# Start addresses of the second layer's SBUF tiles: from 96 bytes past a multiple of 256 to multiples of 256

## The chip, the cores and the metric

The kernel runs on one core of a Trainium2 chip. The metric is device time in microseconds (us) of one execution; the lower the better. TensorE (PE) multiplies matrices. It takes two operands from the on-chip memory SBUF: a stationary one, the weights, which a weight load (PEld) puts in place ahead of the matmul, and a moving one, which streams past it. VectorE (DVE) and ScalarE (ACT) do the elementwise work, GpSimd (POOL) a little of it, and SyncE (SP) issues the transfers (DMA).

## The reference

An attention with a decaying state, then two feed-forward layers on its output, all in float32:

```
B, H, S, D = 4, 8, 768, 48;  tokens 3072, d_model 384, d_ff 2048
for t:   y_t   = r_t @ (state + (u*k_t) v_t^T);   state = w * state + k_t v_t^T
layer 1: h = x @ w_in;  g = max(h, 0) + alpha * min(h, 0);  x2 = g @ w_out
layer 2: h = x2 @ w_in; g = h * tanh(softplus(h));          out = g @ w_out
```

## The kernel before, in words

**Blocks and slots.** The 3072 tokens form six blocks of 512 (NCH = 6). A layer goes through its 2048 inner features in sixteen tiles of 128 (NF = 16). One block with one feature tile is a slot, so each layer has 96 slots. In a slot TensorE forms h for 128 features and 512 tokens (`emit_h`, L229) and later adds the slot's share of the output to accumulators (`mA_out`, L612, in layer 1; `mB_out`, L730 and L732, in layer 2).

**Nine and nine.** Each float32 operand is held as a high and a low part (`hi`, `lo`), and a product is three matmuls: high by high, high by low, low by high. With 384 = 3 x 128 input features, h takes nine matmuls of 128 x 512, and the output takes nine too. Only the last block of layer 2 turns the output product round: there the parts of g are the weights, `w_out` is the moving operand with 384 columns, and a slot has twelve of them (L730).

**Order.** Layer 1 runs slot by slot along the places of a table, with the attention of later tokens between the slots (L433 to L485: many small matmuls, a batch of them every four slots). Layer 2 runs in pairs: the h of two slots, then the outputs of the two slots that lie four slots back (LAG_B = 4). `mish` (L671) puts six ACT and five DVE operations of each slot between h and the output. The places of the instructions are the same in both kernels.

**Homes of the tiles.** A tile gets its place in SBUF from a pool, in the order of creation. Pool `per` lives throughout: the block inputs `x`, the weight tiles `w0` to `w12` of both layers, `w13` to `w15` of layer 1, and the parts `ghi`, `glo` of g in layer 1. Pool `att` holds the attention's tiles. At the end of layer 1 `fin_open` (L627) closes `att` and puts pool `fin` over the same bytes: three constants for ACT's bias operand, the layer 2 tiles `w13`, `w14`, `w15` (W_OWN = 13, L193), the parts of g in four buffers each (`ghiB`, `gloB`, L592), and the tiles `a`, `b`, `s2`, `c`, `s3` and `oo` that TensorE doesn't read. The last slots of layer 1 (from G_3 = 86 on) already write their g to `ghiB` and `gloB`.

A tile of one column takes 32 bytes of a partition. Three of them stand at the start of `fin`, so all that follows starts 96 bytes past a multiple of 256.

Of the kernel before, what the change touches and what calls it, by code (L numbers as in the profile page):

```python
# [21 lines left out]
F32 = mybir.dt.float32  # L22
# [7 lines left out]
B, H, S, D = 4, 8, 768, 48  # L30
# [3 lines left out]
NPR = H // 2  # L34
# [3 lines left out]
PR = 112  # L38
# [93 lines left out]
MK = (32.0 / 768398401.0) ** 0.5  # L132
# [4 lines left out]
def attention_and_two_ff(ctx: ExitStack, tc, rkT, nat, wT, ub, consts, w1, w2, alphaT, out):  # L137
# [8 lines left out]
    att = att_ctx.enter_context(tc.tile_pool(name="att", bufs=1))  # L146
# [88 lines left out]
    oma = per.tile([128, NF], F32, name="oma")  # L235
    wt = att.tile([PR, NPR], F32, name="wt")
    w64 = att.tile([PR, NPR], F32, name="w64")
    cst = att.tile([128, 2 * C], F32, name="cst")
    ubt = att.tile([128, DM], F32, name="ubt")
    ident = cst[:, 0:128]  # L240
# [44 lines left out]

    RK = per.tile([PR, 2, NPR, C], F32, tag="w1", name="RK")
    RKs = att.tile([PR, 2, NPR, C], F32, name="RKs")
    uw = att.tile([PR, NPR, 2], F32, name="uw")
    w96 = att.tile([PR, NPR], F32, name="w96")
    Kn = att.tile([128, 2, NPR, 2, D], F32, name="Kn")  # L290
    T = att.tile([PR, B, NPR, 64], F32, name="T")
    def tables():
# [78 lines left out]
        dve.tensor_tensor(out=rk, in0=rk, in1=w.unsqueeze(2).to_broadcast([PR, 2 * NPR, 2, HC]), op=ALU.mult)  # L371

    def new_c(u):
        return att.tile([128, H, 1], F32, tag="cc", name="cc", bufs=2)

    def c_first(u):

        rk = inp[u][0]
        m = new("g")[0:PR].rearrange("d (p s) -> d p s", p=NPR)
        dve.tensor_tensor(out=m, in0=rk[:, 0], in1=rk[:, 1], op=ALU.mult)  # L380
        y = yt_t[u] = bank(*(("yt",), ("acc1",), ("h", 2), ("h", 2))[u])
        t = y[:, KC * C:KC * C + H]
        for p in range(NPR):
            pe.matmul(t[:, 2 * p:2 * p + 2], m[:, p, :], uw[:, p, :], start=True, stop=True)
        c_t[u] = None, new_c(u)
        act.activation(out=c_t[u][1][:, :, 0].rearrange("s (q p) -> s q p", q=2),
                       in_=t.rearrange("s (p q) -> s q p", q=2), func=AF.Copy)

    def prep_c(u):
        n = inp[u][1]  # L390
        c_t[u] = n[:, 0].rearrange("s (h d) -> s h d", h=H), new_c(u)
        pool.tensor_tensor(out=n[:, 0], in0=n[:, 0], in1=ubt, op=ALU.mult)
        pool.tensor_tensor(out=n[:, 0], in0=n[:, 0], in1=n[:, 1], op=ALU.mult)
# [231 lines left out]
    fin = {}  # L625

    def fin_open():  # L627
        att_ctx.close()
        fin["p"] = ctx.enter_context(tc.tile_pool(name="fin", bufs=1))
        for nm, v in (("half", 0.5), ("m1", -1.0), ("m575", 575.0 * MK)):  # L630
            fin[nm] = fin["p"].tile([128, 1], F32, name=nm)
            pool.memset(fin[nm], v)

    def load_x2(j):
# [15 lines left out]
    v = {}  # L650
# [194 lines left out]
    with tc.manual_schedule():  # L845
# [65 lines left out]
        for f in range(NF):  # L911
# [3 lines left out]
            at(s + 2.69, w_join, (1, f))  # L915
            at(s + 2.69, w2_store, f)
        at(80.69, fin_open)
        at(78.7, load_x2, 0)
        when = [(13, 82.72), (14, 83.4), (0, 83.69), (1, 84.69), (2, 85.69), (15, 86.4), (3, 86.69), (4, 87.69), (5, 88.69),
# [98 lines left out]
```

## Time and profile before

| | |
|---|---|
| median of three runs | 884.35 us (883.03 to 884.73) |
| the profiled execution's own time | 883.32 us |
| its span in the trace | 881.4 us |
| PE busy | 872.5 us, 99% of the span |
| DVE, ACT, POOL busy | 637.8, 608.7, 97.3 us |
| granted TensorE clock | full in all 40 slices of the page |

The span is what the trace covers, from the first instruction to the last; 1.9 us of the profiled execution's time lie around it. Matmuls overlap in the trace: one of 512 columns is recorded with some 0.39 us, and the next starts long before that is over. What a matmul costs is therefore read from start to start.

### The profile page before, as it was taken

To read this page: it belongs to the slowest core of one execution; us is meant where nothing else is said; L and a number is where in the kernel's file an instruction comes from. 1 tells how busy PE (TensorE), PEld (TensorE's weight loads), DVE (VectorE), ACT (ScalarE), POOL (GpSimd) and SP (SyncE) were. 2 spreads that over 40 slices of the span, in tenths; PEclk is the share of its full clock that TensorE was granted. 3 is DMA by queue.
4 is the path that set the end of the run, shared out by engine and by line. 5 is a ranking of instruction groups with operands and counts; after the bars stand their busy time and mean duration, and the time that the engine had idled before them with its cause. 6 is when DMAs were issued, how large, how long until landed. Compare 5 with 4: busy or idle time off the path is not lost.

```text
span 881.4 us, 16867 instructions
## 1 busy us (share of the span) xinstructions
PE 872.5 (99%) x6460; PEld 721.7 (82%) x6460; DVE 637.8 (72%) x1029; ACT 608.7 (69%) x1150; POOL 97.3 (11%) x119
## 2 busy tenths in 40 slices
PE   9899999999999999999999999999999999999998
PEld 8788888888888888888888888888888888888897
DVE  7799856656657566544656887887887887887876
ACT  2677745455445544544555998998998998998886
POOL 3633122111122111100002000000000000000000
PEclk9999999999999999999999999999999999999999
DMA  8975474255444426212620200110110110100101
GB/s 308 277 241 155 133 188 138 85 159 163 137 132 138 140 88 215 64 57 88 189 89 19 108 1 0 27 47 1 28 45 1 27 46 1 25 12 1 24 14 36
DMA packets 65839, 80.40 MB, mean 91 GB/s; under 512 B 39712, under 2 KB 52960, under 8 KB 65760
## 3 DMA queue, kind: packets, MB, share of 16 engines
q1 hardware_dynamic: 65200, 79.24, 30.1%
q8 instruction: 50, 0.82, 0.4%
q14 instruction: 29, 0.24, 0.1%
q10 hardware_dynamic: 560, 0.10, 0.1%
HBM read 61.16 MB, written 15.73 MB: 87 GB/s over the span
## 4 chain that ended last, share of the span: by engine, by line
PE 97%; DVE 1%; ACT 1%; DMA 0%; issue 0%; POOL 0%; DVEq 0%; ACTq 0%; POOLq 0%
PE h L229 44%; PE acc L612 23%; PE sc L732 8%; PE acc L732 8%; PE yt L732 4%; PE acc L730 3%; PE acc L564 2%; PE sc L433 1%; PE sc L730 1%; PE h L464 1%; PE yt L485 1%; PE sc L478 1%; PE yt L464 1%; DMA x2d<-xo 0%; DVE g L380 0%
## 5 line engine op out<-in xcount | busy, mean ns | idle before, releaser
L229 PE MATMUL h<-x,w 128*128 128x512 f32 x1728 | 418.5, 391 | 2.1 <-DVE x L158 1.0
L229 PEld LDWEIGHTS h<-x,w 128*128 128x128 f32 x1728 | 323.9, 188 | 74.5 <-ACT w L155 1.2
L612 PE MATMUL acc<-ghi,w 128*128 128x512 f32 x516 | 175.1, 394 | 0.0
L580 ACT ACTIVATE m<-h 128x512 f32<-128x512 f32 x96 | 57.1, 595 | 91.2 <-PE h L229 91.1
L612 PEld LDWEIGHTS acc<-ghi,w 128*128 128x128 f32 x516 | 96.8, 188 | 21.3
L582 DVE SCALAR_TENSOR_TENSOR g<-m,oma,h 128x512 f32<-128x512 f32 x96 | 71.5, 745 | 57.4 <-ACT m L580 56.4
L155 ACT ACTIVATE ghi<-g 128x512 fp32r<-128x512 f32 x86 | 54.1, 629 | 79.4 <-PE acc L612 43.0
L612 PE MATMUL acc<-glo,w 128*128 128x512 f32 x258 | 100.4, 389 | 0.0
L158 DVE TENSOR_TENSOR glo<-g,ghi 128x512 fp32r<-128x512 f32 x86 | 59.3, 689 | 52.5 <-ACT ghi L155 52.4
L669 DVE SCALAR_TENSOR_TENSOR a<-ghi,h 128x512 f32<-128x512 f32 x96 | 66.0, 687 | 43.0 <-ACT ghi L666 36.1
L677 ACT ACTIVATE m<-h 128x512 f32<-128x512 f32 x96 | 56.3, 587 | 42.3 <-PE h L229 42.3
L669 DVE SCALAR_TENSOR_TENSOR g<-s,c 128x512 f32<-128x512 f32 x95 | 65.1, 686 | 25.3 <-ACT s L666 25.2
L158 DVE TENSOR_TENSOR gloB<-g,ghiB 128x512 fp32r<-128x512 f32 x105 | 71.9, 685 | 7.2 <-ACT ghiB L155 7.2
L666 ACT ACTIVATE ghi<-m,half 128x512 f32<-128x512 f32 x96 | 69.6, 725 | 3.2
L155 ACT ACTIVATE ghiB<-g 128x512 fp32r<-128x512 f32 x105 | 64.8, 617 | 9.2 <-PE acc L612 7.3
L732 PE MATMUL sc<-ghiB,w 128*128 128x512 f32 x192 | 68.1, 395 | 0.0
L666 ACT ACTIVATE glo<-ghi,m 128x512 f32<-128x512 f32 x96 | 68.0, 709 | 0.1
L666 ACT ACTIVATE s<-s,m 128x512 f32<-128x512 f32 x96 | 68.0, 709 | 0.0
L666 ACT ACTIVATE s<-glo,m 128x512 f32<-128x512 f32 x96 | 68.0, 708 | 0.0
L669 DVE SCALAR_TENSOR_TENSOR b<-ghi,a 128x512 f32<-128x512 f32 x96 | 67.2, 701 | 0.1
L669 DVE SCALAR_TENSOR_TENSOR c<-glo,b 128x512 f32<-128x512 f32 x95 | 65.0, 684 | 0.0
L732 PE MATMUL acc<-ghiB,w 128*128 128x512 f32 x192 | 63.0, 395 | 0.0
(193 smaller groups left out, 1167.7 us busy)
## 6 DMA issues: line engine op xcount, KB each, us to landing
wrawr<-in_w SPq DMA_DIRECT2D x24, 768.0 KB, 6.0
nat<-in_nat SPq DMA_DIRECT2D x40, 288.0 KB, 4.3
w2d<-wj SPq DMA_DIRECT2D x16, 384.0 KB, 2.6
wraw<-w2d SPq DMA_DIRECT2D x16, 384.0 KB, 3.0
rk<-in_rkT SPq DMA_DIRECT2D x40, 128.0 KB, 2.9
x2d<-xo SPq DMA_DIRECT2D x6, 768.0 KB, 3.2
x<-x2d SPq DMA_DIRECT2D x6, 768.0 KB, 4.4
rk<-in_rkT SPq DMA_DIRECT2D x40, 96.0 KB, 2.6
```

What stands on the lines that cost most here:

```text
L155: act.activation(out=hi, in_=src, func=AF.Copy)
L158: eng.tensor_tensor(out=lo, in0=src, in1=hi.bitcast(F32), op=ALU.subtract)
L229: pe.matmul(h, w_in(layer, f, a, c), x[:, b, c, :], start=(k == 0), stop=(k == 3 * KC - 1))
L464: pe.matmul(y[i][64 * q:64 * q + 64, p * HC:(p + 1) * HC], T[ROWS[h], 2 * bp + i, k, :], pair[i][ROWS[h], 0, k, t], start=(r == 0 and not ...
L580: act.activation(out=m, in_=hA[s], func=AF.Relu, scale=-1.0)
L582: dve.scalar_tensor_tensor(out=g, in0=m, scalar=oma[:, f:f + 1], in1=hA.pop(s), op0=ALU.mult, op1=ALU.add)
L612: pe.matmul(acc[0][c], w_out(0, f, a)[:, c * 128:(c + 1) * 128], g[b], start=(f == 0 and k == 0), stop=(f == NF - 1 and k == 2))
L666: act.activation(out=out, in_=in_, func=AF.Square, scale=scale, bias=fin[bias])
L669: dve.scalar_tensor_tensor(out=out, in0=in0, scalar=scalar, in1=in1, op0=op0, op1=ALU.mult)
L677: act.activation(out=bnew("t", n), in_=v["h", n], func=AF.Tanh, scale=0.5)
L730: pe.matmul(acc[1][t][:, :DM], g[a][:, t * C:(t + 1) * C], w_out(1, f, b), **se)
L732: pe.matmul(acc[1][t], w_out(1, f, a)[:, t * 128:(t + 1) * 128], g[b], **se)
```

## The change

Three places of the code change the bytes at which tiles start; no instruction is added, taken away or moved on any engine, and no wait changes. In `att`, the small tiles `uw` and `w96` are created earlier and `w96` is 40 columns wide instead of 4 (only the first 4 are used); the small tiles `cc` have four columns a head instead of one. In `fin`, the three bias constants are columns of one tile of 64 columns (256 bytes).

```diff
     w64 = att.tile([PR, NPR], F32, name="w64")
+    uw = att.tile([PR, NPR, 2], F32, name="uw")
+    w96 = att.tile([PR, 40], F32, name="w96")[:, 0:NPR]
     cst = att.tile([128, 2 * C], F32, name="cst")
...
-    uw = att.tile([PR, NPR, 2], F32, name="uw")
-    w96 = att.tile([PR, NPR], F32, name="w96")
...
-        return att.tile([128, H, 1], F32, tag="cc", name="cc", bufs=2)
+        return att.tile([128, H, 4], F32, tag="cc", name="cc", bufs=2)[:, :, 0:1]
...
-        for nm, v in (("half", 0.5), ("m1", -1.0), ("m575", 575.0 * MK)):
-            fin[nm] = fin["p"].tile([128, 1], F32, name=nm)
+        t = fin["p"].tile([128, 64], F32, name="biases")
+        for n, (nm, v) in enumerate((("half", 0.5), ("m1", -1.0), ("m575", 575.0 * MK))):
+            fin[nm] = t[:, n:n + 1]
             pool.memset(fin[nm], v)
```

The first byte of the tiles within a partition, as the two built programs have it, and what is left of it after division by 256 and by 512:

| tiles | before | mod 256 | mod 512 | changed | mod 256 | mod 512 |
|---|---|---|---|---|---|---|
| `x`, `w0` to `w12`, layer 1's `w13` to `w15`, `ghi`, `glo` | 141568 (`x`) | 0 | 256 | the same | 0 | 256 |
| layer 2's `w13` (and `w14`, `w15`) | 176480 | 96 | 352 | 176640 | 0 | 0 |
| `ghiB`, `gloB` (first buffer) | 194912 | 96 | 352 | 195072 | 0 | 0 |
| attention: `rk`, `nat`, `T` (`rk`) | 190336 | 128 | 384 | 190464 | 0 | 0 |
| attention: `Ah` | 220608 | 192 | 448 | 220928 | 0 | 256 |
| `cst` | 176448 | 64 | 320 | 176640 | 0 | 0 |

The slices that TensorE takes of these tiles begin whole multiples of 512 bytes further on in the feed-forward layers (128 columns of 4 bytes), so that they have the same remainders as their tiles.

## Rows read from the trace of the kernel before

**Rows 1.** The page: the span, and PE's busy time, share and instructions.

```profile
span 881.4 us, 16867 instructions
...
PE 872.5 (99%) x6460; PEld 721.7 (82%) x6460; DVE 637.8 (72%) x1029; ACT 608.7 (69%) x1150; POOL 97.3 (11%) x119
```

**Rows 2.** Who waited for whom from 440 us on: total, times, longest.

```profile
ACT m L677 <- PE h L229: 42.3, 47, 3.0
...
PEld acc L730 <- DVE gloB L158: 0.2, 1, 0.2
```

**Rows 3.** Windows: stretch, its length, busy time and instructions of each engine, clock.

```profile
403.30:444.08 40.78, 40.78 (x181) 33.77 (x180) 24.11 (x33) 21.71 (x35) 0.00 (x0) 1.00 0.43 140
444.08:823.32 379.24, 379.24 (x1639) 307.67 (x1638) 299.75 (x467) 325.58 (x541) 6.53 (x4) 1.00 0.11 27
823.32:881.40 58.08, 54.53 (x283) 50.11 (x281) 42.28 (x68) 45.70 (x77) 0.00 (x0) 0.99 0.12 27
```

**Rows 4.** Timeline of PE, end of layer 1: start, length, matmuls merged.

```profile
431.84 2.20 PE L229 MATMUL h<-x,w 128*128 128x512 f32 x9
...
433.88 0.39 PE L612 MATMUL acc<-ghi,w 128*128 128x512 f32 x1
...
435.92 2.20 PE L229 MATMUL h<-x,w 128*128 128x512 f32 x9
...
444.08 0.40 PE L612 MATMUL acc<-ghiB,w 128*128 128x512 f32 x1
...
446.19 4.28 PE L229 MATMUL h<-x,w 128*128 128x512 f32 x18
...
450.31 0.40 PE L612 MATMUL acc<-ghiB,w 128*128 128x512 f32 x1
```

**Rows 5.** Timeline of PE in layer 2, around a change of blocks.

```profile
594.24 4.36 PE L229 MATMUL h<-x,w 128*128 128x512 f32 x18
...
598.44 0.39 PE L732 MATMUL acc<-ghiB,w 128*128 128x512 f32 x1
...
602.64 4.28 PE L229 MATMUL h<-x,w 128*128 128x512 f32 x18
...
606.76 0.40 PE L732 MATMUL acc<-ghiB,w 128*128 128x512 f32 x1
...
617.38 0.39 PE L732 MATMUL acc<-gloB,w 128*128 128x512 f32 x1
...
618.74 0.39 PE L732 MATMUL acc<-gloB,w 128*128 128x512 f32 x1
```

**Rows 6.** Timeline of PE in layer 2's last block.

```profile
823.32 0.51 PE L730 MATMUL acc<-w,ghiB 128*128 128x384 f32 x2
...
827.49 4.28 PE L229 MATMUL h<-x,w 128*128 128x512 f32 x18
...
831.61 0.51 PE L730 MATMUL acc<-w,ghiB 128*128 128x384 f32 x2
...
852.35 4.34 PE L229 MATMUL h<-x,w 128*128 128x512 f32 x18
...
856.53 0.52 PE L730 MATMUL acc<-w,ghiB 128*128 128x384 f32 x2
...
860.77 4.38 PE L229 MATMUL h<-x,w 128*128 128x512 f32 x18
...
864.99 0.52 PE L730 MATMUL acc<-w,ghiB 128*128 128x384 f32 x2
```

**Rows 7.** Timeline of PE in layer 1, from the end of an attention batch.

```profile
264.21 0.50 PE L612 MATMUL acc<-ghi,w 128*128 128x512 f32 x1
264.55 0.39 PE L612 MATMUL acc<-glo,w 128*128 128x512 f32 x1
...
266.40 2.21 PE L229 MATMUL h<-x,w 128*128 128x512 f32 x9
```

**Rows 8.** Groups of ACT from 500 to 600 us, and two of the page: busy, mean ns, idle before.

```profile
L677 ACT ACTIVATE m<-h 128x512 f32<-128x512 f32 x24 | 14.1, 587 | 9.6 <-PE h L229 9.6
...
L155 ACT ACTIVATE ghi<-g 128x512 fp32r<-128x512 f32 x86 | 54.1, 629 | 79.4 <-PE acc L612 43.0
...
L155 ACT ACTIVATE ghiB<-g 128x512 fp32r<-128x512 f32 x105 | 64.8, 617 | 9.2 <-PE acc L612 7.3
```

## The prediction

> **What bounds the kernel now.** I read the page first: PE is busy 872.5 of 881.4 us [rows 1]. Then the list of waits: from 440 us on no row of it has PE's matmuls waiting; one weight load waits once, for 0.2 us, while ACT waits 42.3 us for PE [rows 2]. So from there to nearly the end the time is the number of matmuls times what one costs from start to start. The clock column is 1.00 throughout both long stretches [rows 3], so nothing is to be had from the clock. The question is what a matmul costs, and where it costs more.
>
> For that I read PE's timeline, start to start. At the end of layer 1, from 431.84 to 435.92 us, one slot's nine h matmuls and nine output matmuls take 2.04 + 2.04 = 4.08 us [rows 4], which is 4.08 / 18 = 226.7 ns each. The stretch up to 444.08 keeps that pace: 180 weight loads in 40.78 us [rows 3] (that count is exact; the count of matmuls has one more, which overlaps the edge). At 444.08 the first output product reads `ghiB` and `gloB`, and this one alone takes until 446.19: 2.11 us instead of 2.04 [rows 4]. The instructions have the same shapes and the same weights' tiles as before; `mish` hasn't begun. What differs is the home of g. From there to the last block, 1638 matmuls take 379.24 us [rows 3], or 231.5 ns each: 4.9 ns more than before 444.08.
>
> Layer 2's timeline says which ones pay. Two h slots whose weights start on a multiple of 256 take 4.12 us (602.64 to 606.76), but the two with `w14` and `w15` take 4.20 (594.24 to 598.44) [rows 5]: moving operand on the multiple, weights 96 past it. Output products of slots with weights on the multiple, where g is 96 past it, also take 4.20 (598.44 to 602.64). And where both lie 96 past, with `w15` in the output product, six matmuls take 617.38 to 618.74 = 1.36 us, 226.7 ns again [rows 5]. So it is the mixture of remainders between the two operands that costs, (4.20 - 4.08) / 18 = 6.7 ns a matmul, not the odd start as such. The 0.04 us that an h pair takes over 4.08 is a settling: after a break the stream runs some nine matmuls before it is back at its pace. It also shows after an attention batch, where the first matmul takes 0.34 us and the nine together 2.19 instead of 2.04 [rows 7], and after the 384-column products of the last block, 827.49 to 831.61 = 4.12 us [rows 6].
>
> **The change, part by part.** *The tiles of `fin`.* After the change both operands of every 512-column matmul of the feed-forward layers start on a multiple of 256. If all run at 226.7 ns, the long stretch of 1638 = 91 x 18 matmuls takes 91 x 4.08 = 371.28 us instead of 379.24 [rows 3, 4]: 7.96 us less. The check by kinds agrees roughly: some 970 mixed matmuls (90 output products at the end of layer 1, 720 in layer 2, 18 slots of h with nine each) at 6.7 ns are 6.5 us, and the settling of some 45 pairs at 0.04 us makes up the rest, less the products with `w15` that already run at pace. I take 7.96, since it is read off a whole stretch.
>
> *The last block.* Its 384-column products already run at 24 in 4.17 us (823.32 to 827.49), or 174 ns, although their weights lie 96 past and the moving `w_out` does not; nothing to gain there. The h pair of tiles 12 and 13 takes 852.35 to 856.53 = 4.18 and could take 4.12 with its settling; the products with `w13` take 856.53 to 860.77 = 4.24 and could take 4.17; the h pair of 14 and 15 takes 860.77 to 864.99 = 4.22 and could take 4.12 [rows 6]. Sum 0.23 us. The settling after each run of 384 columns stays.
>
> *The tiles of `att`.* The attention's tiles lay on multiples of 64 or 128 and now lie on 256. Bounds: nothing, or at most the settling after each of the 20 batches. Of the 2.19 - 2.04 = 0.15 us the first matmul has 0.34 - 0.23 = 0.11 [rows 7], which is the change of shapes; what is left is 0.04, so 20 x 0.04 = 0.8 us. I take nothing, because the same settling follows the 384-column products, where every tile of the h pair already lies on 256. The 0.8 goes into the lower end.
>
> *The constants in one tile, `uw`, `w96`, `cc`.* The same memsets and activations with the same waits: nothing. A transfer into a tile with another start costs nothing to PE, because no row of the waits from 440 us on has PE waiting for one [rows 2]; if that cover went, the earliest victim would be a block's input, which is loaded many slots ahead.
>
> *What is late next.* ACT waits for PE before the first activation of each slot: 9.6 us for 24 slots, 0.40 us a slot [rows 8]. A slot falls from 379.24 / 91 = 4.17 to 4.08, so 0.31 us of cover is left. The tiles that ACT writes move too. The nearest rows are the same copy into `ghi` on a multiple of 256, 629 ns, and into `ghiB` 96 past it, 617 ns [rows 8]; if each of the six activations of a slot grew by these 12 ns it would be 0.07 us, still under cover. ACT would decide only from 0.31 / 6 = 52 ns an operation. DVE works behind ACT and waits for it.
>
> **A rule against it.** The rows show 231.5 ns against 226.7 ns a matmul with the home of g as the only difference at 444.08 [rows 3, 4]. The Trainium skill, "TensorE: Matmul & The Clock Gate", section "Step-by-step: what each phase is for", says that the weight load and the moving stream have separate read ports into SBUF, so that loading the next weights takes nothing from the running matmul. By that rule the two operands' remainders would have nothing to do with each other, and the change would give nothing; the rows, where the cost depends on the pair, speak against it. The same page's section "Back-to-back issue gap" gives about N / 2.4 + 2.5 ns, so an estimate from that page of 216 ns for 512 columns; if starts on 256 brought that, the stretch would fall to about 354 us, but layer 1 has all its tiles there and shows 226.7.
>
> The sum by rows: 7.96 + 0.23 = 8.2 us. The profiled execution took 883.32 us, so it would take 875.1 us with a span of 873.2; the median of the runs lies 1.03 above that execution, so 884.35 - 8.2 = 876.1 us.
>
> **The rivals.** *Remainders after 512 count.* In layer 1 all operands have the remainder 256 after 512; after the change `ghiB`, `gloB` and `w13` to `w15` have 0, and `x` and the other weights still 256. No pair of rows shows 0 against 256. If that mixes as 96 did, every matmul that pays now pays then: 884.3. If it costs half, 880.3. For it: the reference pace of 226.7 was only ever seen with equal remainders. Against it: the 384-column products mix remainders and run without loss [rows 6], and slices 512 bytes apart within a weight tile make no difference in h [rows 4].
>
> *Starts don't matter; layer 2 is slower for another reason*, such as ACT and DVE reading SBUF more densely. Then 884.3 too. Against it: the step at 444.08 before layer 2, and the products with `w15` at full pace in the midst of it [rows 4, 5]. The Trainium skill, "SBUF — State Buffer", section "Specifications (TRN2)", gives lines of 16 bytes as what an access has to stay in; 96 is six of them, so by that rule this rival would be right and the time unchanged.
>
> *Slower.* A distance of 256 could be worse than one of 96: the two streams could meet on the same part of SBUF all along. Place: the output products of layer 2 and h with `w13` to `w15`. If the extra doubled from 6.7 to 13.4 ns, the 970 matmuls would add 6.5 us: 890.9. It decides as soon as a mixed matmul costs more than the 233.4 ns (226.7 + 6.7) of now. Nothing in the rows speaks for it but the lack of such a pair.
>
> **How the numbers follow.** All at pace 0.77 (876.1, own range 874.9 to 877.6: the 0.8 of the attention below, some settling that stays above); half 0.06; remainders after 512 at full cost 0.06; another reason 0.05; slower 0.06. The range must reach the half case and may leave out the rest (0.17): 874.9 to 880.5. A measurement here tells 0.2%, 1.8 us, from no change. Faster 0.77 + 0.06 = 0.83; the same 0.06 + 0.05 = 0.11; slower 0.06.
>
> **What would show it.** Right: from the first product with `ghiB` to the first with 384 columns, the same 1638 weight loads in about 371.3 us; h pairs of layer 2 at 4.08 us whatever the tile, with `w14` and `w15` too; output pairs at 4.08; ACT's wait for h down to some 0.3 us a slot; layer 1 up to 444 us as it was. Wrong: output pairs still at 4.20 while h pairs of tiles 0 to 11 fall to 4.08 or not (remainders after 512); pairs over 4.20 (slower); a row in which PE waits for DVE or ACT in layer 2; a settling that disappears after the attention's batches (0.8 us more than I count).

## The result, and the profile after

The changed kernel takes 876.91 us (median of six runs) against 883.87 us of the kernel before (six runs): a ratio of 0.992, with an interval from 0.9906 to 0.9935. One run of each six was in a slow state (1755.98 and 1451.08 us), and the ratio leaves it out. Measured once more in the experiments it gave 876.13 against 884.04 us, ratio 0.9902 (0.9885 to 0.992). Forecast were 876.1 us, or a ratio of 876.1 / 884.35 = 0.9907.

The page of the changed kernel, to be laid beside [rows 1]:

```profile
span 875.1 us, 16867 instructions
...
PE 864.6 (99%) x6460; PEld 721.4 (82%) x6460; DVE 639.5 (73%) x1029; ACT 608.9 (70%) x1150; POOL 95.3 (11%) x119
```

The number of instructions is the same, and so is nearly all of DVE's and ACT's work; PE's busy time fell by 7.9 us. The view of windows cuts the execution at the first output product with `ghiB` and at the first one with 384 columns (columns as in [rows 3]):

```profile
0.00:445.88 445.88, 438.91 (x4540) 363.88 (x4541) 296.86 (x496) 237.69 (x535) 89.30 (x115) 1.00 0.49 154
445.88:817.16 371.28, 371.28 (x1639) 307.43 (x1638) 300.35 (x467) 325.53 (x541) 5.99 (x4) 1.00 0.11 27
817.16:875.10 57.94, 54.46 (x283) 50.12 (x281) 42.30 (x68) 45.69 (x77) 0.00 (x0) 1.00 0.12 27
```

The same 1638 weight loads took 379.24 us before and take 371.28 now: 7.96 us less, the forecast to the second decimal. The last stretch lost 58.08 - 57.94 = 0.14 us. The first one, where the forecast was no change, is 445.88 - 444.08 = 1.80 us longer in this execution; the experiments come back to it.

PE's timeline in layer 2, the same slots as in [rows 5]:

```profile
592.76 4.24 PE L229 MATMUL h<-x,w 128*128 128x512 f32 x18
...
596.84 0.39 PE L733 MATMUL acc<-ghiB,w 128*128 128x512 f32 x1
...
600.92 4.24 PE L229 MATMUL h<-x,w 128*128 128x512 f32 x18
...
605.00 0.39 PE L733 MATMUL acc<-ghiB,w 128*128 128x512 f32 x1
```

The h pair with `w14` and `w15` (592.76 to 596.84) takes 4.08 us instead of 4.20, the output pair behind it 4.08 instead of 4.20, the next h pair 4.08 instead of 4.12. With no mixed products ahead of it there is nothing left to settle.

ACT from 500 to 600 us, the group that waits for PE:

```profile
L678 ACT ACTIVATE m<-h 128x512 f32<-128x512 f32 x25 | 14.7, 588 | 7.5 <-PE h L229 7.5
```

Its wait fell from 0.40 to 7.5 / 25 = 0.30 us a slot [rows 8]. ACT still waits for PE, so PE sets the time as before.

### The profile page after: what moved, and what is told of

The parts are those of the page before. It is cut to its first block, busy times and chain, and to the rows that moved or that the text cites. A ratio compares the mean times of both kernels' runs of the same rounds, so it can differ in the third digit from the quotient of the medians.

```text
span 875.1 us, 16867 instructions
## 1 busy us (share of the span) xinstructions
PE 864.6 (99%) x6460; PEld 721.4 (82%) x6460; DVE 639.5 (73%) x1029; ACT 608.9 (70%) x1150; POOL 95.3 (11%) x119
## 4 chain that ended last, share of the span: by engine, by line
PE 97%; DVE 1%; ACT 1%; issue 0%; DMA 0%; POOL 0%; DVEq 0%; ACTq 0%; POOLq 0%
PE h L229 44%; PE acc L612 23%; PE sc L733 7%; PE acc L733 7%; PE yt L733 4%; PE acc L731 3%; PE acc L564 1%; PE sc L433 1%; PE sc L731 1%; PE h L464 1%; PE yt L485 1%; PE sc L478 1%; PE yt L464 1%; DMA x2d<-xo 0%; DVE g L380 0%
## 5 line engine op out<-in xcount | busy, mean ns | idle before, releaser
L667 ACT ACTIVATE ghi<-m,biases 128x512 f32<-128x512 f32 x96 | 69.6, 725 | 3.2
L667 ACT ACTIVATE glo<-ghi,biases 128x512 f32<-128x512 f32 x96 | 68.1, 710 | 0.1
L667 ACT ACTIVATE s<-glo,biases 128x512 f32<-128x512 f32 x96 | 68.1, 709 | 0.0
L667 ACT ACTIVATE s<-s,biases 128x512 f32<-128x512 f32 x96 | 68.0, 708 | 0.0
```

Source lines behind the costliest of these rows:

```text
L667: act.activation(out=out, in_=in_, func=AF.Square, scale=scale, bias=fin[bias])
```

## The experiments

**One half of the change alone.** The constants in one tile, the attention's tiles where they were:

```diff
-            fin[nm] = fin["p"].tile([128, 1], F32, name=nm)
+        t = fin["p"].tile([128, 64], F32, name="biases")
...
+            fin[nm] = t[:, n:n + 1]
```

> Only the constants of layer 2 stand in one tile of 256 bytes; the attention's tiles start where they did before. Theory (the second layer's and the last ten output products' operands with equal remainders run at 226.7 ns a matmul, and nothing else of the change matters): the 1638 weight loads from the first product with ghiB on take 371.3 us, the time falls by 8.2 us from the kernel before, about as the whole change does or better by up to 1 us. Rival (the moved attention tiles cost about 1 us in layer 1, which is why the whole change gave 7.0 us and not 8.2): this kernel is about 1 us faster than the whole change, near 875.7. Rival (the difference is only that of the starting stretch from one execution to the next): no difference to the whole change that its spread allows to tell.

Measured: 876.11 us against 885.39 of the kernel before, ratio 0.9894 (0.988 to 0.9908). Its windows:

```profile
0.00:444.71 444.71, 438.28 (x4540) 363.97 (x4541) 295.90 (x496) 237.21 (x535) 90.50 (x115) 1.00 0.50 154
444.71:815.99 371.28, 371.28 (x1640) 307.53 (x1638) 300.33 (x467) 325.48 (x541) 5.99 (x4) 1.00 0.11 27
```

The long stretch is the same to the hundredth as with the whole change, so its 7.96 us need this half alone. The rest of the 9.28 us by which the medians differ is not placed: the kernel before stood at 885.39 us in this measurement, at 883.87 and 884.04 in the two others.

**The other half alone.** The attention's tiles on multiples of 256 (`uw`, `w96` and `cc` as in the change), the constants as before.

> Only the attention's tiles start on multiples of 256; the three constants of layer 2 are tiles of their own again, so ghiB, gloB and w13 to w15 lie 96 past. Theory: no change from the kernel before (ratio 1.000 within 0.1%), the long stretch takes 379.2 us again. Rival (attention tiles gain): up to 0.8 us less, the nine products after a batch in 2.15 us or less. Rival (they cost): about 1 us more, 885.

Measured: 883.88 us against 885.39, ratio 0.9984 (0.9973 to 0.9994). The long stretch:

```profile
444.73:823.98 379.25, 379.25 (x1640) 307.67 (x1639) 299.91 (x467) 325.66 (x541) 6.54 (x4) 1.00 0.11 27
```

It is back at its old length. The ratio's interval lies just below 1, so that the 0.1% of the expectation was missed (0.16%). The trace has no place for a gain: up to the first product with `ghiB` PE takes 444.73 us against 444.08, and from one output product of layer 1 to another, with ten attention batches between them, it takes 184.73 us here (162.37 to 347.10), in the kernel before and in the repeat of the change (both 161.68 to 346.41). The 1.5 us between the medians stay unplaced.

**Both operands off.** If each operand had to start on a multiple, shifting everything by 96 bytes would be the worst case; if only the two against each other count, it costs nothing. A pad ahead of all tiles does it, on top of the whole change:

```diff
+    per.tile([128, 24], F32, name="pad")
     al = per.tile([128, NF], F32, name="al")
```

> A pad of 96 bytes ahead of every tile: all operands of all feed-forward matmuls start 96 past a multiple of 256, in layer 1 too. Theory of the pair (only the remainders of the two operands against each other count): full pace, 226.7 ns everywhere, 4.08 us for each slot of layer 1 and pair of layer 2, time as that of the whole change, about 877. Rival of the start itself (each operand that starts 96 past costs, whatever the other does): 1584 matmuls of layer 1 pay 6.7 ns as well, about 10 us above the kernel before, 894.

Measured: 875.62 us in one execution.

```profile
0.00:444.49 444.49, 438.30 (x4540) 363.88 (x4541) 294.69 (x496) 237.18 (x535) 90.76 (x115) 1.00 0.51 154
444.49:815.77 371.28, 371.28 (x1640) 307.43 (x1638) 300.34 (x467) 325.48 (x541) 5.99 (x4) 1.00 0.12 27
```

Layer 1 does not suffer (444.49 us with all its operands 96 past, 444.08 before) and the long stretch is at full pace. No feed-forward operand starts on a multiple of 256 here. The excess of the kernel before is gone, so alignment as such is not the cause; a distance of 0 between the two remainders is enough. This rival of the start itself forecast 894 us and has fallen.

**Other distances.** The whole change with a longer tile of constants, so that `ghiB`, `gloB` and `w13` to `w15` lie 64, 128 or 32 bytes past a multiple of 256, with `x` and the other weights on one:

```diff
-        t = fin["p"].tile([128, 64], F32, name="biases")
+        t = fin["p"].tile([128, 80], F32, name="biases")
```

(96 columns for a distance of 128, 72 for 32.)

> The whole change, but the tile of constants is 64 bytes longer, so ghiB, gloB and w13 to w15 start 64 past a multiple of 256. If a remainder of 64 bytes is what counts: full pace, about 877, long stretch 371.3 us. If multiples of 128 or 256 are needed: a matmul of mixed remainders costs some 6.7 ns more, about 885, long stretch 379.

> ghiB, gloB and w13 to w15 start 128 past a multiple of 256, all else as in the whole change. A distance of 64 already cost 4.9 us over the long stretch (376.20 against 371.28 us). If the distance counts to a multiple of 128: 371.3 us, as with 0. If it counts to a multiple of 256: between 373 and 379 us.

> ghiB, gloB and w13 to w15 start 32 past a multiple of 256. If what counts is whether the distance is an odd multiple of 32: as with 96, 379.2 us. If the cost grows with the distance: less than the 376.2 us of 64. If 32 bytes still lie within what is read at once: 371.3 us.

Measured, one execution each: 882.87, 881.23 and 886.02 us. The windows of the long stretch, first with a distance of 64:

```profile
445.69:821.88 376.19, 376.19 (x1639) 307.52 (x1638) 300.37 (x467) 325.59 (x541) 5.98 (x4) 1.00 0.11 27
```

With a distance of 128:

```profile
443.80:820.88 377.08, 377.08 (x1639) 307.61 (x1638) 299.85 (x467) 325.57 (x541) 6.55 (x4) 1.00 0.11 27
```

With a distance of 32:

```profile
447.08:825.23 378.15, 378.15 (x1639) 307.38 (x1638) 299.87 (x467) 325.88 (x541) 6.54 (x4) 1.00 0.11 27
```

The stretches are compared, and not the totals, because what lies ahead of them differed from execution to execution (443.80 to 447.08 us). Over 371.28 us the stretch costs 6.87 us with 32, 4.91 with 64, 7.96 with 96 (the kernel before) and 5.80 with 128. The whole change itself has a distance of 256 in all its output products of layer 2 with `w0` to `w12` (0 against 256 after division by 512) and costs nothing. So the distance counts to a multiple of 256 as far as these show: none of the four smaller ones is free, and the cost doesn't simply grow with it. The expectation for 32 left out what happened, which lies between the values it named for 64 and for 96.

Pair by pair the order is simpler. PE's timeline with a distance of 64, first an output pair whose g lies 64 past its weights, then the h pair with `w14` and `w15`, whose weights lie 64 past `x`:

```profile
582.15 0.40 PE L733 MATMUL acc<-ghiB,w 128*128 128x512 f32 x1
...
586.29 4.35 PE L229 MATMUL h<-x,w 128*128 128x512 f32 x18
...
594.61 4.36 PE L229 MATMUL h<-x,w 128*128 128x512 f32 x18
...
598.81 0.39 PE L733 MATMUL acc<-ghiB,w 128*128 128x512 f32 x1
```

The output pair takes 4.14 us, the h pair 4.20. With 32, 96 and 128 both kinds take 4.19 to 4.22 us in the same place. So an unequal pair costs nearly the same at every distance tried, but for one case: at 64 it also counts which of the two operands lies further on. The rest of the differences is in the equal h pairs between the unequal output pairs: 4.12 us with 96, up to 4.13 with 64, about 4.10 with 32 and with 128.

**Only g, or only the weights.** A pad behind `w15` puts `ghiB` and `gloB` alone 96 past; with the old constants and another pad, `w13` to `w15` alone:

```diff
     def g_late(tag):
+        if "pad" not in fin:
+            fin["pad"] = fin["p"].tile([128, 24], F32, name="pad")
```

(40 columns in the second kernel.)

> A pad of 96 bytes between w15 and ghiB: layer 2's w13 to w15 start on multiples of 256, ghiB and gloB 96 past. Theory of the pair: every output product with 512 columns is mixed, those with w13 to w15 too, and all h matmuls are matched: some 810 x 6.7 = 5.4 us and the settling of the 49 h pairs that follow, 1.9 us, so the long stretch takes about 378.6 us; h pairs with w14 and w15 take 4.12 us, output pairs with w14 and w15 4.20. Theory of the start: the excess of w13 to w15 is gone, that of g stays whole, and this excess and that of the kernel with only the weights moved add up to 7.96 us.

> The weights w13 to w15 of layer 2 start 96 past, ghiB and gloB on multiples of 256. Theory of the pair: h with w13 to w15 is mixed (18 slots of 9, 1.1 us) and so are the output products with them (15 slots of 9, 0.9 us), with some settling after: long stretch about 373.5 us, output pairs with w14 and w15 4.20 us; the excess of this kernel and of the one with only g moved add up to more than 7.96 us, about 9.5. Theory of the start: 1.1 us of h alone, 372.4 us, or with the products 373.3, and the two add up to 7.96.

Measured: 882.91 and 882.36 us in one execution each. The long stretch with g alone off:

```profile
443.84:823.08 379.24, 379.24 (x1639) 307.66 (x1638) 299.89 (x467) 325.55 (x541) 6.53 (x4) 1.00 0.11 27
```

With the weights alone off:

```profile
446.71:820.33 373.62, 373.62 (x1640) 307.58 (x1638) 300.25 (x467) 325.47 (x541) 5.99 (x4) 1.00 0.11 27
```

With g alone off, PE's timeline has the h pair with `w14` and `w15`, and later the output pair with the same weights:

```profile
593.96 4.28 PE L229 MATMUL h<-x,w 128*128 128x512 f32 x18
...
598.08 0.40 PE L735 MATMUL acc<-ghiB,w 128*128 128x512 f32 x1
...
614.75 0.40 PE L735 MATMUL acc<-ghiB,w 128*128 128x512 f32 x1
...
618.96 3.37 PE L229 MATMUL h<-x,w 128*128 128x512 f32 x14
```

The h pair takes 4.12 us (4.20 in the kernel before), the output pair 4.21. The excesses are 7.96 and 2.34 us, together 10.30, though the kernel before, which has both off, pays only 7.96. Moving the weights onto multiples while g stays off gains nothing at all: what h with these weights wins, the products of g with them lose, since there the two had been equal. That is what the theory of the pair says and what a cost of each start by itself can't give. Its number for the weights was right (373.5), that for g 0.6 us low: it took 4.20 us for every output pair, and behind an equal h pair they take 4.21 or 4.22, because an unequal run needs some matmuls to settle too.

**The same cost put into layer 1.** The whole change, with `ghi` and `glo` alone off by 96 bytes:

```diff
     def new(tag, n=512, dt=F32, bufs=1):
+        pad = tag in ("ghi", "glo") and tag not in padded
+        if pad:
+            padded.add(tag)
+            per.tile([128, 24], F32, name=tag + "_before")
...
+        if pad:
+            per.tile([128, 40], F32, name=tag + "_behind")
```

> The whole change, with ghi and glo of layer 1 put 96 past a multiple of 256 while x, w0 to w15 and all of layer 2 stay on multiples. Theory of the pair: the 86 output products of layer 1 that read ghi and glo are mixed and take 2.115 us instead of 2.04, and the h that follows each takes 2.078 by its settling: 86 x 0.113 = 9.7 us more before the first product with ghiB, a slot of layer 1 takes 4.19 us; layer 2's stretch stays at 371.3; about 886.5 in all. If layer 2 were slow for another reason than the starts: no change from the whole change.

Measured: 882.72 us in one execution. PE's timeline in layer 1, and then the windows:

```profile
413.52 2.24 PE L238 MATMUL h<-x,w 128*128 128x512 f32 x9
...
415.60 0.40 PE L621 MATMUL acc<-ghi,w 128*128 128x512 f32 x1
...
417.72 2.24 PE L238 MATMUL h<-x,w 128*128 128x512 f32 x9
```

```profile
0.00:451.19 451.19, 445.42 (x4541) 363.38 (x4541) 296.22 (x496) 238.19 (x535) 90.52 (x115) 1.00 0.48 152
451.19:822.47 371.28, 371.28 (x1640) 307.54 (x1638) 300.32 (x467) 325.55 (x541) 5.99 (x4) 1.00 0.11 27
```

The slot goes from 4.08 to 417.72 - 413.52 = 4.20 us, as expected: 2.08 for h with its settling and 2.12 for the mixed product. Layer 2 stays at 371.28. So the cost follows the operands wherever they are, and layer 2 as such has nothing to do with it. The sum over layer 1 was oversized: 451.19 - 444.05 = 7.14 us beside the second measurement of the change, not 9.7. Some 0.8 us of the difference belong to the execution: its first product with `ghi` starts at 47.34 us, that of the change at 48.11. Most of the rest lies in the slots behind an attention batch, which settle anyway [rows 7]: there the nine output products take 2.20 us where they took 2.19, and the h behind them 2.17 where it took 2.13. They were counted as if they had been at full pace.

**Once more, side by side.** The change, its half with the constants, and all tiles off by 96, in five rounds on one chip.

> The whole change once more. The long stretch takes 371.28 us again. What is open is the time before it: 445.88 us in the profiled execution of the change, 444.08 in that of the kernel before. If the execution makes the difference (a wait for PE's code near 46 us and a clock that fell after it): the stretch ahead of the first product with ghiB lies between 443.8 and 447.1 us, as in the other kernels, and the time is that of the change with the constants alone within 0.2%. If the attention's tiles cost: 445.5 us or more, and 0.7 us or more behind the kernel with the constants alone.

> The constants of layer 2 in one tile, attention as before, beside the whole change on the same chip. If the execution makes the difference: the same time as the whole change within 0.2%. If the attention's tiles cost: 0.7 us or more faster. If they gain: slower.

> All tiles that TensorE reads 96 past a multiple of 256, now with rounds. Theory of the pair: the same time as the whole change within 0.2%, about 876.

Measured: 876.13, 876.13 and 878.14 us against 884.04; ratios 0.9902 (0.9885 to 0.992), 0.99 (0.9881 to 0.9919) and 0.992 (0.9903 to 0.9938). The windows of the whole change, this time:

```profile
0.00:444.05 444.05, 437.93 (x4541) 363.58 (x4541) 296.11 (x496) 237.41 (x535) 90.28 (x115) 1.00 0.49 155
444.05:815.33 371.28, 371.28 (x1640) 307.43 (x1638) 300.30 (x467) 325.52 (x541) 5.99 (x4) 1.00 0.11 27
815.33:873.30 57.97, 54.45 (x283) 50.11 (x281) 42.30 (x68) 45.70 (x77) 0.00 (x0) 1.00 0.12 27
```

The first stretch is 444.05 us, what it was in the kernel before, and the span of 873.3 us is 0.1 from the 873.2 forecast; that it is so near is luck in part, since the first stretch ran from 443.80 to 447.08 us in the executions of this case. The moved attention tiles neither cost nor gain: beside the half with the constants alone, the medians are the same. The kernel with all tiles off came out 0.23% behind, a little more than the 0.2% that was expected to hold; its windows show where in this execution:

```profile
446.65:817.93 371.28, 371.28 (x1640) 307.54 (x1638) 300.35 (x467) 325.53 (x541) 5.99 (x4) 1.00 0.12 27
817.93:877.80 59.87, 54.47 (x283) 50.13 (x281) 42.30 (x68) 45.69 (x77) 0.00 (x0) 0.98 0.13 26
```

Not in the long stretch: 2.6 us ahead of it, and 1.9 us in the last one. Of the latter PE has nothing: it is busy for 54.47 us there (54.45 in the change), and the rest comes after its last matmul. The kernel with the weights alone off, whose layer 1 has its tiles on multiples of 256, has the same two delays: 446.71 us ahead of the long stretch, and behind it

```profile
820.33:880.40 60.07, 54.59 (x283) 50.23 (x281) 42.27 (x68) 45.70 (x77) 0.00 (x0) 0.98 0.12 26
```

So neither delay needs all tiles off by 96, and the first execution of that kernel had neither. Whether its addresses make them more frequent is open.

No experiment gave a version that is faster than the change by more than the noise; the half with the constants alone does the same with less.

## Why the prediction was right

**The pace of a matmul.** The step on which all hung, that the mixture of the operands' remainders costs and the matched pace is 226.7 ns, held in every run: 7.96 us forecast and measured in the long stretch, and the experiments with equal remainders of 96, with g or the weights alone, and with layer 1 mixed each moved the cost where the pair said. Why unequal remainders cost is open; no run looks behind the pace.

**The check by kinds.** It was weaker than it looked. Of the 720 output products of layer 2 that it counted, the 135 with `w13`, `w14` and `w15` had equal remainders, not those with `w15` alone. And three of the 18 h slots lie in the last block, outside the stretch. That leaves 90 + 585 + 135 = 810 unequal matmuls and about 5.4 + 1.8 = 7.2 us; the missing 0.8 us are settling, which the unequal runs have too. The forecast did not rest on it: 7.96 was read off the whole stretch.

**Remainders after 512.** This rival is out: 0 against 256 costs nothing. The other one, that starts don't matter, is out as well, and with it, for this kernel, what was drawn from two rules of the Trainium skill, that the time would stay. "TensorE: Matmul & The Clock Gate", section "Step-by-step: what each phase is for", has the weight load and the moving stream on separate read ports, the one taking nothing from the other; here the pace depends on where the two start against each other, 371.28 against 379.24 us for the same work. And the 16-byte lines of "SBUF — State Buffer", section "Specifications (TRN2)", are no measure for it: distances of 32, 64, 96 and 128 bytes, all multiples of 16, cost 4.91 to 7.96 us.

**Slower.** The rival of a worse collision at a distance of 256 did not come: those products run at 226.7 ns.

**The last block.** Forecast 0.23 us, measured 0.14 and 0.11 (57.94 and 57.97 against 58.08). The term left something out: the 384-column products of the changed kernel are a little slower. Its timeline has 24 of them in 821.35 - 817.16 = 4.19 us, 0.02 more than in [rows 6], and the three runs of 24 after that take 0.01 or 0.02 more as well; that they settle in their turn behind h at full pace is a guess.

```profile
817.16 0.51 PE L731 MATMUL acc<-w,ghiB 128*128 128x384 f32 x2
...
821.35 4.28 PE L229 MATMUL h<-x,w 128*128 128x512 f32 x18
```

The h pair after them, 821.35 to 825.47, still takes 4.12 us: the settling stays, as forecast. One row was misread: the products from 856.53 to 860.77 in [rows 6] are those with `w8` and `w9`, four slots back, and not with `w13`. Their operands have the same remainders as those of the runs at 4.17 us, so why they took 4.24 is open; in the changed kernel it is gone all the same (850.39 to 854.57, 4.18 us).

**The attention.** Taken as nothing, and it was nothing: ten batches and forty slots take 184.73 us with its tiles moved and without. The 0.8 us of settling behind its batches, kept for the lower end, was not to be had.

**The scatter.** The first measurement gave 7.0 us, the second 7.9, the sum said 8.2. The long stretch is the same in every profiled execution with equal remainders; what differs lies ahead of it or behind PE's last matmul. In the first profiled execution of the change PE waited 1.8 us in an attention batch, and its clock fell behind it. The row of the waits, then windows from 44 to 52 us:

```profile
PE yt L485 <- issue: 1.8, 1, 1.8
```

```profile
44.00:46.00 2.00, 1.30 (x94) 1.15 (x84) 1.90 (x3) 1.47 (x2) 0.04 (x1) 1.00 0.67 147
46.00:48.00 2.00, 0.89 (x32) 0.81 (x33) 2.00 (x4) 0.00 (x0) 0.00 (x0) 1.00 0.55 157
48.00:50.00 2.00, 2.00 (x19) 1.63 (x14) 1.65 (x2) 1.64 (x4) 0.00 (x0) 0.68 1.07 242
50.00:52.00 2.00, 2.00 (x6) 1.52 (x6) 1.45 (x3) 2.00 (x7) 1.24 (x2) 0.50 0.98 346
```

PE was busy for 2.19 of the 4 us up to 48, and then the granted clock went to 0.50, the lower of its two levels (1.2 GHz): six matmuls in 2 us instead of ten in the kernel before. In the repeat the same wait lasted 1.0 us and the clock stayed at 1.00. The wait belongs to the execution and not to the addresses: the change itself had 1.8 and 1.0 us of it, all tiles off by 96 had 1.0 and 1.8, the kernel before 0.2. The wait alone doesn't bring the clock down, since all tiles off by 96 waited 1.8 us at a clock of 1.00. What ends it is not shown as such. But in each of the twelve executions that have the wait, it ends 1.3 to 1.8 us after a 16 KB packet of the page's instruction queue (q8) has ended, which speaks for a wait for instructions; whose instructions that packet brings isn't shown. A second place is at about 106 us, where PE waits 1.1 us for DVE in four executions with different addresses (the attention's half alone, a distance of 64, the weights alone off, and all tiles off by 96 the second time) and not in the kernel before or the change.

## What to carry to other kernels

When matmuls are back to back, compare the first bytes of the stationary and the moving operand after division by 256: equal remainders ran at 226.7 ns for 128 x 512 here, with new weights for every matmul, unequal ones at 230 to 234, and a few small tiles at the start of a pool are enough to shift everything behind them. Aligning one side alone can gain nothing, because it unmatches the pairs that were equal. The step in PE's start-to-start times at the instruction where a tile's home changes shows it, while the busy share (99% before and after) and the mean durations on the page do not: in the kernel before 394 ns for products of layer 1 with `ghi` at full pace, 395 for the unequal ones of layer 2.

## What was not expected of the hardware

That the absolute start doesn't matter was expected from six matmuls in [rows 5] only; all tiles 96 bytes off at full pace (371.28 us) makes it plain. The cost does not follow the distance in order: 6.87, 4.91, 7.96 and 5.80 us for 32, 64, 96 and 128 bytes. An unequal pair costs about the same at all of them, but for the one with g 64 past its weights. Why the 384-column products of the kernel before paid nothing for theirs is open; with a distance of 128 a run of 24 did pay, 4.24 us instead of 4.17. The pace itself returns only over some nine matmuls after each break seen here (an attention batch, a run of 384 columns, an unequal run), which costs h about 0.04 us each time and is the reason why matched h slots between mixed products were slow too.
